# The order of the fallback's flag on VectorE in a fused attention and mixture-of-experts kernel

## Chip, cores and metric

The kernel runs on one core of one Trainium2 chip. The metric is device time in microseconds (us) of one execution, given as the median of several runs. Engines are called by the names of the profile: PE is TensorE's matmul, PEld its weight load, DVE is VectorE, ACT is ScalarE, POOL is GpSimd, SP is SyncE, which here issues the loads and stores.

## What is computed

The reference is attention with a few sink keys and a sliding window, and behind it a mixture of experts that keeps at most `capacity` tokens for each expert:

```
B, H, S, D = 4, 8, 768, 64          # n_sink 4, window 128
scores = q @ k.T / sqrt(D)          # keep: key < n_sink, or 0 <= query - key < window
a = softmax(where(keep, scores, -1e9));   x = a @ v         # x: 3072 tokens x 512
logits = x @ w_gate                 # 8 experts
expert = argmax(logits);  gate = softmax(logits)[expert]
for each expert: keep the 80 tokens (capacity) with the largest gate
    out[token] = gate * (relu(x[token] @ w1[e]) @ w2[e])    # 512 -> 1024 -> 512
```

`n_sink`, `window` and `capacity` come as 64-bit integers in device memory.

## The kernel before, in words

The kernel is built for 4 sinks, a window of 128 and a capacity of up to 80. It computes the output for these numbers, and at the very end it branches to a general and slow version, `any_window`, if a flag says that the numbers are others. The flag needs only the three numbers.

Attention runs in 48 ticks. A tick handles two units; a unit is a block of 128 queries for a pair of heads. The ticks are pipelined by hand: in tick n TensorE computes the scores of tick n (`scores`, L551), turns the probabilities of tick n-1 (L604), and weighs the values of tick n-2 (`weighted`, L639 and L645); in between stand the gate's small matmuls and, in ticks 8 and 9 among others, the turning of finished rows (`rows_turn`, L678). For each unit VectorE copies masked scores inside PSUM (L571) and takes the row maximum `nm` (`softmax`, L578), ScalarE makes the exponentials `prob` (`exps`, L588). GpSimd copies the sinks' probabilities (`sink_probs`, L596 and L597) when the exponentials of a tick are done, and then masks the turned probabilities (`own_probs`, L624, and `before_probs`, L631). The next scores go into the same two PSUM buffers, so TensorE's scores of tick n+1 wait for the exponentials of tick n.

The loop over the ticks stands inside a manual schedule: each engine takes its instructions in the order in which the code writes them. Work that comes up once is put into a calendar: `at((6, "dve end"), f)` calls f in tick 6 behind the softmax of that tick, and "pool" is the place on GpSimd between `sink_probs` and `own_probs`. Entries of the calendar that matter here: `pick_row` is cleared at the end of tick 5 on VectorE (L986), GpSimd makes the picks from it in tick 7 (`make_picks`, L512) and scales the next queries in the same place (`scale_q`, L428), and `read_numbers` stands at the end of tick 6. It turns the integers `ints`, loaded by three small transfers (L489), into floats: a cast (L517), L519, L520, and L521, which writes `prm`. `cut_slots` (tick 9) reads `prm` too.

The flag's five instructions (L1431 to L1434 and L1436, each on one element) are written at the end of the program, behind the manual schedule, so a scheduler puts them where they can run.

Behind the ticks come the ranking of the tokens, the gathers, and from about 203 us the experts' two matrix products, with the weights loaded by SP along the way.

Of the kernel before, what the change touches and what calls it, by code (L numbers as in the profile page):

```python
# [8 lines left out]
F32 = mybir.dt.float32  # L9
F32R = mybir.dt.float32r  # L10
BF16 = mybir.dt.bfloat16
I32 = mybir.dt.int32
I8 = mybir.dt.int8
AF = mybir.ActivationFunctionType
ALU = mybir.AluOpType
# [12 lines left out]
SINK, WIN, CAP = 4, 128, 80  # L28
# [215 lines left out]
def attention_moe(ctx: ExitStack, tc, q, k, v, n_sink, window, w_gate, w1, w2, capacity, q_t, k_t, v_t, vs_t, wg_t, out):  # L244
    nc = tc.nc
    ve, ac, po, pe = nc.vector, nc.scalar, nc.gpsimd, nc.tensor

    const = ctx.enter_context(tc.tile_pool(name="const", bufs=1))
# [79 lines left out]
    with ExitStack() as actx:  # L328
# [159 lines left out]
        for n, a in enumerate((n_sink, window, capacity)):  # L488
            nc.sync.dma_start(ints[:, n, :], a.bitcast(I32).partition_broadcast(P))  # L489
        prm = const.tile([P, 3], F32, name="prm")  # L490

        def make_experts():
            po.iota(e_down, pattern=[[-1, E]], base=E, channel_multiplier=0, allow_small_or_imprecise_dtypes=True)
            po.tensor_scalar(p_bits, e_down, float(8 << 23), float(87 << 23), ALU.mult, ALU.add)
# [20 lines left out]
        def read_numbers():  # L515
            intf = const.tile([P, 3, 2], F32, name="intf")
            ve.tensor_copy(intf, ints)  # L517
            wrap = const.tile([P, 3, 2], F32, name="wrap")
            ve.tensor_scalar(wrap[:, :, 0:1], intf[:, :, 0:1], 0.0, 4294967296.0, ALU.is_lt, ALU.mult)  # L519
            ve.scalar_tensor_tensor(wrap[:, :, 1:2], intf[:, :, 1:2], 4294967296.0, wrap[:, :, 0:1], ALU.mult, ALU.add)  # L520
            ve.tensor_tensor(prm[:, :, None], wrap[:, :, 1:2], intf[:, :, 0:1], ALU.add)  # L521

        def cut_slots():

            past = const.tile([P, CAP], F32, name="past")
            ve.tensor_scalar(past, slot_row, prm[:, 2:3], EMPTY, ALU.is_ge, ALU.mult)
            ve.tensor_tensor(slot_row, slot_row, past, ALU.add)
# [453 lines left out]
        def at(n, f, *args):  # L981
            cal.setdefault(n, []).append((f, args))
# [20 lines left out]
        at((5, "dve end"), ve.memset, pick_row, 1.0)  # L1003
        at((4, "pool"), make_ties)
        at((7, "pool"), make_picks)
        at((6, "dve end"), read_numbers)
        at((9, "dve end"), cut_slots)
        for b in range(B):
            s = b * NPB * NPAIR
            if b + 1 < B:  # L1010
                at(s + 4, load_v, b + 1)
                at(s + 5, load_k, b + 1)
                for n, m in enumerate((0, 2, 1, 3)):
                    at((s + 6 + n, "act end"), round_v, b + 1, m)
                    at((s + (8 if n < 2 else 12), "pool"), split_v, b + 1, m)
# [411 lines left out]
        chain.close()  # L1427

    fast.close()
    flag = const.tile([1, 3], F32, name="flag")  # L1430
    ve.tensor_scalar(flag[:, 0:1], prm[0:1, 0:1], float(SINK), None, ALU.not_equal)  # L1431
    ve.scalar_tensor_tensor(flag[:, 1:2], prm[0:1, 1:2], float(WIN), flag[:, 0:1], ALU.not_equal, ALU.max)
    ve.scalar_tensor_tensor(flag[:, 0:1], prm[0:1, 2:3], 0.0, flag[:, 1:2], ALU.is_lt, ALU.max)
    ve.scalar_tensor_tensor(flag[:, 1:2], prm[0:1, 2:3], float(CAP), flag[:, 0:1], ALU.is_gt, ALU.max)  # L1434
    other = const.tile([1, 1], I32, name="other")
    ve.tensor_copy(other, flag[:, 1:2])  # L1436
    with tc.If(nc.values_load(other, min_val=0, max_val=1) > 0):  # L1437
        any_window(tc, q, k, v, w_gate, w1, w2, prm, ident, out)

# [51 lines left out]
```

## Time and profile before

| what | value |
|---|---|
| median of 3 runs | 296.15 us (295.87 to 297.26) |
| the profiled execution's own time | 294.72 us |
| its span, first to last instruction | 293.0 us |
| mean granted clock of TensorE, share of full | 0.982 |
| busy: PE, DVE, ACT, POOL | 268.8, 171.0, 166.4, 160.5 us |

Busy shares tell which engine has the most work, not which one is late at a given moment. For a step of a pipeline like this one the way to read is: find an idle time of the engine with the most work, see what ended it, and go back through the engine that was waited for until one is found that was busy. The rows of a timeline give start, duration, engine, line, what is written and read, and in brackets an idle time in front with what ended it.

### The profile page before, as it was taken

Reading aid. Unit: us, or ns where it says so; the run is one execution under the profiler, and the core shown is the slowest. Engines: PE = TensorE matmul, PEld = TensorE weight load, DVE = VectorE, ACT = ScalarE, POOL = GpSimd, SP = SyncE. Lnnn points to the kernel's source line nnn. Section 1 sums busy time; section 2 is a strip of 40 time slices with the busy share of each in tenths; the row PEclk is TensorE's granted clock in tenths of the full one; section 3 lists DMA queues with packets and bytes.
Section 4 is the critical chain, followed back from the end, with each engine's and each line's share of the span. In section 5 each row is a group of like instructions: output and inputs, shape, how many; then the busy total and the mean of one; then the engine's idle time right before and its main releaser. Section 6 shows DMA issues by size and latency. Waiting matters only on the chain. (4 is left out here: it accounts for less than half of the span.)

```text
span 293.0 us, 11250 instructions
## 1 busy us (share of the span) xinstructions
PE 268.8 (92%) x4390; PEld 210.5 (72%) x4390; DVE 171.0 (58%) x566; ACT 166.4 (57%) x670; POOL 160.5 (55%) x365
## 2 busy tenths in 40 slices
PE   8889699999999999999989999985999999999991
PEld 3556577676777667667667667643999999998980
DVE  7678878696989888989997897880000000000001
ACT  3867687878987888687578777730112122212210
POOL 5866768758888768769757686735212021001111
PEclk9999799999999999999999999999899999999997
DMA  6989643597880999855184915594989989999811
GB/s 164 371 296 354 241 145 145 213 321 248 273 287 4 293 269 409 333 182 185 63 296 143 347 53 177 173 346 165 311 246 303 298 296 293 312 331 287 279 37 34
DMA packets 33366, 69.76 MB, mean 238 GB/s; under 512 B 4250, under 2 KB 6426, under 8 KB 32922
## 3 DMA queue, kind: packets, MB, share of 16 engines
q1 hardware_dynamic: 32282, 66.34, 66.8%
q0 software_dynamic: 1024, 2.62, 3.0%
q8 instruction: 37, 0.61, 0.9%
q14 instruction: 23, 0.19, 0.2%
HBM read 55.05 MB, written 13.89 MB: 235 GB/s over the span
## 5 line engine op out<-in xcount | busy, mean ns | idle before, releaser
L588 ACT ACTIVATE prob<-sc,nm 128x132 f32<-128x132 f32 (+1 forms) x192 | 68.9, 375 | 12.2 <-DVE nm L578 11.9
L551 PE MATMUL sc<-kv,q 64*64 64x196 f32 (+2 forms) x768 | 48.1, 337 | 9.3 <-ACT prob L588 7.3
L551 PEld LDWEIGHTS sc<-kv,q 64*64 64x64 f32 x768 | 21.5, 133 | 30.7 <-ACT prob L588 19.4
L578 DVE TENSOR_REDUCE nm<-sc 128x2 f32<-128x264 f32 (+1 forms) x96 | 41.4, 431 | 3.3
L571 DVE COPY_PREDICATED sc<-upper,sc 128x256 f32<-128x256 int8 x80 | 33.7, 422 | 14.6 <-PE sc L551 7.5
L616 ACT COPY pt<-pp 128x512 f32<-128x512 f32 x48 | 28.1, 585 | 24.8 <-PE pp L604 19.9
L588 ACT ACTIVATION_READ_ACCUMULATOR prob<-sc,nm 128x1 f32 x192 | 40.3, 210 | 0.0
L1342 DVE COPY xs<-px 128x320 f32<-128x320 f32 x7 | 3.4, 491 | 58.4 <-PE px L1337 51.6
L645 PE MATMUL xp<-pt,kv 128*64 128x128 f32 x384 | 37.4, 287 | 0.0
L624 POOL TENSOR_SCALAR_AFFINE_SELECT own<-pt 128x512 f32<-128x512 f32 (+1 forms) x48 | 27.6, 575 | 11.7 <-ACT pt L616 11.3
L1411 POOL DMA_INDIRECT out_dram<-y,idx x8 | 7.4, 922 | 46.8 <-ACT y L1405 42.9
L604 PE MATMUL pp<-ident,prob 128*128 128x128 f32 x192 | 31.9, 289 | 0.1
L645 PE MATMUL xp<-own,kv 128*64 128x128 f32 x320 | 31.3, 274 | 0.0
L631 POOL TENSOR_SCALAR_AFFINE_SELECT pt<-pt 128x512 f32<-128x512 f32 (+1 forms) x48 | 28.5, 593 | 3.3
L604 PEld LDWEIGHTS pp<-ident,prob 128*128 128x128 f32 x192 | 20.5, 143 | 13.6 <-issue 9.1
L1359 PE MATMUL ph<-xs,w 128*64 128x80 f32 x640 | 27.6, 242 | 0.3 <-issue 0.2
L695 POOL TENSOR_TENSOR xr<-xr,rs 128x512 f32<-128x512 f32 x21 | 22.4, 1067 | 7.7 <-ACT xr L683 7.6
L1359 PEld LDWEIGHTS ph<-xs,w 128*64 128x64 f32 x640 | 25.3, 145 | 0.7 <-issue 0.3
L1377 PE MATMUL py<-h,w 128*64 128x80 f32 x640 | 24.8, 234 | 0.6 <-ACT yt L1388 0.6
L1363 ACT ACTIVATE h<-ph 128x320 f32<-128x320 f32 x16 | 7.0, 437 | 31.4 <-PE ph L1359 31.4
L1377 PEld LDWEIGHTS py<-h,w 128*64 128x64 f32 x640 | 23.1, 137 | 1.6 <-issue 0.8
L645 PEld LDWEIGHTS xp<-pt,kv 128*64 128x64 f32 x384 | 21.4, 138 | 3.5 <-POOL pt L631 0.2
(194 smaller groups left out, 520.7 us busy)
## 6 DMA issues: line engine op xcount, KB each, us to landing
w<-in_moe_w_dram SPq DMA_DIRECT2D x80, 256.0 KB, 4.9
kv_w<-in_moe_w_dram SPq DMA_DIRECT2D x48, 256.0 KB, 4.9
kv<-in_v_t_dram SPq DMA_DIRECT2D x12, 512.0 KB, 8.6
out_dram<-zeros SPq DMA_DIRECT2D x24, 256.0 KB, 5.3
x_rows<-xr SPq DMA_DIRECT2D x24, 256.0 KB, 2.2
q<-in_q_t_dram SPq DMA_DIRECT2D x11, 512.0 KB, 3.8
kv<-in_k_t_dram SPq DMA_DIRECT2D x3, 1584.0 KB, 8.3
kv<-in_k_t_dram SPq DMA_DIRECT2D x2, 528.0 KB, 6.7
```

The lines of the kernel that those rows point to most:

```text
L551: pe.matmul(sc[m * D:(m + 1) * D, h, c0:c1], qs[g][r, hp, q0:q0 + D], ks[b][r, hp, k0 + c0:k0 + c1], start=True, stop=True, skip_group_che ...
L571: ve.copy_predicated(own, upper, sc[:, :, 0:P])
L578: ve.tensor_reduce(out=nm, in_=sc[:, :, lo_c:hi_c], axis=AX.X, op=ALU.max, negate=True)
L588: ac.activation(prob[:, a, h, p0:], sc[:, h, lo_c:hi_c], AF.Exp, bias=nm[:, h:h + 1], scale=1.0, accum_out=ssum[:, n, 2 * hp + h:2 * hp + ...
L604: pe.transpose(pp[:, a, h], prob[:, a, h, SINK:], ident)
L616: ac.copy(pt, st.pop((t, "pp")))
L624: po.affine_select(out=own[:, a0:], in_=pt[:, a0:], pattern=[[0, 2 - a0], [0, 2], [1, P]], compare_op=ALU.is_ge, fill=0.0, base=0, channel ...
L631: po.affine_select(out=pt[:, a0:], in_=pt[:, a0:], pattern=[[0, 2 - a0], [0, 2], [-1, P]], compare_op=ALU.is_gt, fill=0.0, base=0, channel ...
L645: pe.matmul(xp[h * D:(h + 1) * D, a * P:(a + 1) * P], val[:, (2 * hp + h) * D:(2 * hp + h + 1) * D], pr[:, a, h], start=False, stop=(a == ...
L695: po.tensor_tensor(xr, xr, gst[(i0, "rs")][:, n, :, None].to_broadcast([P, H, D]), ALU.mult)
L1359: pe.matmul(ph[m * D:(m + 1) * D, f], columns(0, e, c, fc * P + m * D), x[:, c], start=(c == 0 and not (wide and f)), stop=(c == DC - 1), ...
L1377: pe.matmul(to[m * D:(m + 1) * D, dc], columns(1, e, k, dc * P + m * D), h[:, k], start=(k == 0), stop=(k == HC - 1), skip_group_check=True)
```

## The change

The tiles `flag` and `other` are allocated early, the flag's five instructions become a function `judge_numbers`, and the calendar calls `read_numbers` at the end of tick 5 (behind the clearing of `pick_row`) and `judge_numbers` at the end of tick 6. The instructions themselves are the same ones, and the branch at the end reads the same tile.

```diff
         prm = const.tile([P, 3], F32, name="prm")
+        flag = const.tile([1, 3], F32, name="flag")
+        other = const.tile([1, 1], I32, name="other")
...
+        def judge_numbers():
+            ve.tensor_scalar(flag[:, 0:1], prm[0:1, 0:1], float(SINK), None, ALU.not_equal)
+            ve.scalar_tensor_tensor(flag[:, 1:2], prm[0:1, 1:2], float(WIN), flag[:, 0:1], ALU.not_equal, ALU.max)
+            ve.scalar_tensor_tensor(flag[:, 0:1], prm[0:1, 2:3], 0.0, flag[:, 1:2], ALU.is_lt, ALU.max)
+            ve.scalar_tensor_tensor(flag[:, 1:2], prm[0:1, 2:3], float(CAP), flag[:, 0:1], ALU.is_gt, ALU.max)
+            ve.tensor_copy(other, flag[:, 1:2])
...
-        at((6, "dve end"), read_numbers)
+        at((5, "dve end"), read_numbers)
         at((9, "dve end"), cut_slots)
+        at((6, "dve end"), judge_numbers)
...
     fast.close()
-    flag = const.tile([1, 3], F32, name="flag")
-    ve.tensor_scalar(flag[:, 0:1], prm[0:1, 0:1], float(SINK), None, ALU.not_equal)
-    ve.scalar_tensor_tensor(flag[:, 1:2], prm[0:1, 1:2], float(WIN), flag[:, 0:1], ALU.not_equal, ALU.max)
-    ve.scalar_tensor_tensor(flag[:, 0:1], prm[0:1, 2:3], 0.0, flag[:, 1:2], ALU.is_lt, ALU.max)
-    ve.scalar_tensor_tensor(flag[:, 1:2], prm[0:1, 2:3], float(CAP), flag[:, 0:1], ALU.is_gt, ALU.max)
-    other = const.tile([1, 1], I32, name="other")
-    ve.tensor_copy(other, flag[:, 1:2])
     with tc.If(nc.values_load(other, min_val=0, max_val=1) > 0):
```

In the order of the built programs, VectorE before, from the end of tick 5 on (`nm_6_0` is the row maximum of tick 6, unit 0; the last number of a name counts buffers):

```order
L986 MEMSET pick_row_130 128x1280
L571 COPY_PREDICATED sc_0_156<-upper_160,sc_0_156 128x2x128
L578 TENSOR_REDUCE nm_6_0_495<-sc_0_156 128x2
L571 COPY_PREDICATED sc_1_157<-upper_160,sc_1_157 128x2x128
L578 TENSOR_REDUCE nm_6_1_500<-sc_1_157 128x2
L517 CAST intf_529<-ints_185 128x6
L519 TENSOR_SCALAR wrap_531<-intf_529 128x3
L520 SCALAR_TENSOR_TENSOR wrap_531<-intf_529,wrap_531 128x3
L521 TENSOR_TENSOR prm_189<-wrap_531,intf_529 128x3
L1431 TENSOR_SCALAR flag_5113<-prm_189 1x1
L1432 SCALAR_TENSOR_TENSOR flag_5113<-prm_189,flag_5113 1x1
L1433 SCALAR_TENSOR_TENSOR flag_5113<-prm_189,flag_5113 1x1
```

The same place on VectorE in the changed kernel (its line numbers are its own):

```order
L995 MEMSET pick_row_130 128x1280
L519 CAST intf_474<-ints_185 128x6
L521 TENSOR_SCALAR wrap_476<-intf_474 128x3
L522 SCALAR_TENSOR_TENSOR wrap_476<-intf_474,wrap_476 128x3
L523 TENSOR_TENSOR prm_189<-wrap_476,intf_474 128x3
L580 COPY_PREDICATED sc_0_156<-upper_160,sc_0_156 128x2x128
L587 TENSOR_REDUCE nm_6_0_503<-sc_0_156 128x2
L580 COPY_PREDICATED sc_1_157<-upper_160,sc_1_157 128x2x128
L587 TENSOR_REDUCE nm_6_1_508<-sc_1_157 128x2
L526 TENSOR_SCALAR flag_190<-prm_189 1x1
L527 SCALAR_TENSOR_TENSOR flag_190<-prm_189,flag_190 1x1
L528 SCALAR_TENSOR_TENSOR flag_190<-prm_189,flag_190 1x1
```

The four instructions of the numbers moved from behind the softmax of tick 6 to in front of it; the flag's stand in the same place before and after, ahead of the softmax of tick 7.

GpSimd in ticks 6 and 7, before (masks of tick 5, sinks of tick 6, the picks, the scaling of the third group of queries, masks of tick 6):

```order
L624 AFFINE_SELECT own_5_505<-pt_5_492 128x512
L631 AFFINE_SELECT pt_5_492<-pt_5_492 128x512
L596 CAST stk_0_120<-prob_6_494 128x4x2x4
L597 TENSOR_TENSOR stk_0_120<-prob_6_494,stk_0_120 128x4x2x4
L512 AFFINE_SELECT pick_row_130<-pick_row_130 128x1280
L428 TENSOR_SCALAR q_2_272<-q_2_272 128x1024
L624 AFFINE_SELECT own_6_579<-pt_6_555 128x512
```

And in the changed kernel:

```order
L633 AFFINE_SELECT own_5_513<-pt_5_500 128x512
L640 AFFINE_SELECT pt_5_500<-pt_5_500 128x512
L605 CAST stk_0_120<-prob_6_502 128x4x2x4
L606 TENSOR_TENSOR stk_0_120<-prob_6_502,stk_0_120 128x4x2x4
L514 AFFINE_SELECT pick_row_130<-pick_row_130 128x1280
L428 TENSOR_SCALAR q_2_274<-q_2_274 128x1024
L633 AFFINE_SELECT own_6_586<-pt_6_562 128x512
```

Nothing moved here, and nothing moved on TensorE, ScalarE and SP either.

## Rows read from the trace of the kernel before

**Rows 1.** The page, granted clock in 40 slices, tenths of full speed

```profile
PEclk9999799999999999999999999999899999999997
```

**Rows 2.** Waits: engine, line, releaser; us in all, times, longest

```profile
PE sc L551 <- ACT prob L588: 7.3, 18, 2.1
```

**Rows 3.** Stretches: busy us and instructions of each engine, clock, DMA share, GB/s

```profile
core 0: us, PE busy (x) PEld busy (x) DVE busy (x) ACT busy (x) POOL busy (x), PEclk, DMA share, GB/s
34.00:35.00 1.00, 1.00 (x6) 1.00 (x5) 0.93 (x5) 0.51 (x2) 0.84 (x2) 0.50 0.15 55
...
205.00:293.00 88.00, 80.54 (x2090) 77.20 (x2086) 4.54 (x10) 15.11 (x31) 11.91 (x13) 0.97 0.78 252
```

**Rows 4.** Timeline, PE: the scores of ticks 7 to 10, 15 and 17

```profile
26.85 0.93 PE L551 MATMUL sc<-kv,q 64*64 64x196 f32 x16
...
32.05 0.56 PE L551 MATMUL sc<-kv,q 64*64 64x196 f32 x8 [2.11 <-ACT prob L588]
...
37.23 0.90 PE L551 MATMUL sc<-kv,q 64*64 64x196 f32 x16
...
40.45 0.98 PE L551 MATMUL sc<-kv,q 64*64 64x196 f32 x16
...
57.45 0.45 PE L551 MATMUL sc<-kv,q 64*64 64x64 f32 x8
...
64.15 1.11 PE L551 MATMUL sc<-kv,q 64*64 64x196 f32 x16
```

**Rows 5.** Timeline, DVE: from the end of tick 5 to the softmax of tick 7

```profile
22.49 1.12 DVE L986 MEMSET pick_row<- 128x1280 bf16 x1 [0.21 <-issue]
24.33 0.43 DVE L571 COPY_PREDICATED sc<-upper,sc 128x256 f32<-128x256 int8 x1 [0.72 <-ACT xt L655]
...
25.95 0.53 DVE L517 CAST intf<-ints 128x6 f32<-128x6 int32 x1
26.52 0.17 DVE L519 TENSOR_SCALAR wrap<-intf 128x3 f32<-128x3 f32 x1
26.72 0.48 DVE L520 SCALAR_TENSOR_TENSOR wrap<-intf,wrap 128x3 f32<-128x3 f32 x1
...
27.42 0.14 DVE L1431 TENSOR_SCALAR flag<-prm 1x1 f32<-1x1 f32 x1
27.60 0.21 DVE L1432 SCALAR_TENSOR_TENSOR flag<-prm,flag 1x1 f32<-1x1 f32 x1
27.84 1.24 DVE L1433 SCALAR_TENSOR_TENSOR flag<-prm,flag 1x1 f32<-1x1 f32 x1
29.11 0.98 DVE L1434 SCALAR_TENSOR_TENSOR flag<-prm,flag 1x1 f32<-1x1 f32 x1
...
30.21 0.43 DVE L571 COPY_PREDICATED sc<-upper,sc 128x256 f32<-128x256 int8 x1
```

**Rows 6.** Timeline, POOL: masks of ticks 4 and 5, picks, scaling, mask of tick 6

```profile
23.20 0.64 POOL L631 TENSOR_SCALAR_AFFINE_SELECT pt<-pt 128x512 f32<-128x512 f32 x1
...
25.82 0.64 POOL L624 TENSOR_SCALAR_AFFINE_SELECT own<-pt 128x512 f32<-128x512 f32 x1 [1.37 <-ACT pt L616]
26.52 0.66 POOL L631 TENSOR_SCALAR_AFFINE_SELECT pt<-pt 128x512 f32<-128x512 f32 x1
...
27.75 1.32 POOL L512 TENSOR_SCALAR_AFFINE_SELECT pick_row<-pick_row 128x1280 bf16<-128x1280 bf16 x1
29.05 1.04 POOL L428 TENSOR_SCALAR q<-q 128x1024 f32<-128x1024 f32 x1
30.06 0.63 POOL L624 TENSOR_SCALAR_AFFINE_SELECT own<-pt 128x512 f32<-128x512 f32 x1
```

**Rows 7.** Timeline, ACT: the first exponentials of ticks 6 and 7

```profile
25.64 0.38 ACT L588 ACTIVATE prob<-sc,nm 128x132 f32<-128x132 f32 x1
...
31.14 0.37 ACT L588 ACTIVATE prob<-sc,nm 128x132 f32<-128x132 f32 x1 [2.09 <-DVE nm L578]
```

**Rows 8.** Instructions of tile ints: the last of three issues on SP, and their landing

```profile
L489 SPq DMA_DIRECT2D ints<-in_moe_capacity_dram x1: 327/327/327, 11.5 to 11.5; - x1
...
DMA to landing us min/median/max: 8.3/8.6/9.0
```

## Prediction

> **What bounds the kernel now.** I read the page first, then the waits, then one pause engine by engine. The profiled execution took 294.72 us, 1.72 us of it around a span of 293.0 us; the median of the runs shown is 296.15 us, 1.43 us above the profiled one. TensorE's granted clock is at the full level (2.4 GHz) in nearly all of the span, and one of the few slices that fall short is the sixth, 29.3 to 36.6 us [rows 1]. The list of waits gives score matmuls (L551) that waited for ScalarE's exponentials 18 times, 7.3 us in all, the longest 2.1 us [rows 2]: more than a quarter in one place. TensorE's own rows show where. The scores of tick 7 start at 26.85, those of tick 8 only at 32.05, after 2.11 us of idling; behind it the clock stands at half, 1.2 GHz (0.50 at 34 to 35 us), and tick 8 takes until 37.23 [rows 3, 4]. Tick 9, with the same matmuls at the full clock, takes 37.23 to 40.45, 3.22 us; tick 8 took 5.18 [rows 4].
>
> Back along the pause: ScalarE waited 2.09 us for the row maximum of tick 7 and started the exponentials at 31.14 [rows 7]. VectorE, which makes that maximum, was not idle; it did not start tick 7's softmax before 30.21, although the scores of tick 7 were there at 26.85 + 0.93 = 27.78 [rows 4, 5]. From 25.95 to 30.21 it worked at the four instructions that read the numbers (L517 to L521) and the five of the flag [rows 5]. These are 128x6, 128x3 and 1x1 elements, so their length is not work. The fitting view is GpSimd's rows beside them: the flag's third instruction (27.84 + 1.24 = 29.08) ends with make_picks (27.75 + 1.32 = 29.07), its fourth (29.11 + 0.98 = 30.09) with scale_q (29.05 + 1.04 = 30.09); the cast of the numbers ends at 26.48 with own_probs (26.46), the third number instruction at 27.20 with before_probs (27.18) [rows 5, 6]. So a VectorE instruction with two tiles in SBUF, or a wider cast, that starts beside a running GpSimd instruction ends with that one; the flag's first, with one tile as its input, took 0.14 us and was not held [rows 5].
>
> The Trainium skill says the same in "SBUF — State Buffer", section "Who interferes with whom": the pair of ports that the two engines share is locked for a whole instruction by the one that comes first, and a VectorE instruction with two SBUF inputs, or in a two-port mode, needs it. The trace agrees, to 0.02 us in the four places above. Without that rule the 1.24 and 0.98 us would belong to the instructions themselves and would move with them; that reading is the second rival below.
>
> **The change, part by part.** *Removed behind tick 6:* the four number instructions. They took 25.95 to 27.42 there, 1.47 us [rows 5]. The order shows the flag's five instructions where they stood, between the softmax of tick 6 and that of tick 7, and nothing different on the other four engines. What matters is therefore not where the flag stands but that it starts 1.47 us earlier against GpSimd's row of work.
>
> *Added behind tick 5:* the same four, between the memset of pick_row and the softmax of tick 6. The memset ends at 22.49 + 1.12 = 23.61, and before the softmax of tick 6 at 24.33 VectorE idled 0.72 us [rows 5]. Their price, step by step: the cast starts at 23.64 and is held until before_probs of tick 4 ends at 23.20 + 0.64 = 23.84 [rows 6], so to 23.86; L519 0.17 to 24.06; L520, as short as the flag's second, 0.21, to 24.30, or held by one of GpSimd's short instructions until about 24.5; L521 the rest, 27.20 to 27.42 or 0.22, to 24.5 or 24.7 [rows 5]. The softmax of tick 6 then starts 0.15 to 0.35 us late. At worst cast and L520 are as long as they were, 0.53 and 0.48, and all four take 1.47 us: it starts at 25.1, 0.8 us late. Below nothing this price cannot go, since nothing in front of that softmax is taken away. What is queued behind: tick 6's two copies and two maxima, and for them ScalarE. Its exponentials of tick 6 start at 25.64 with no idle time listed, so ScalarE was busy until then [rows 7], while half of the softmax (24.33 to 25.95) was done by about 25.2 [rows 5]. That slack of 0.4 us hides 0.15 to 0.35; the second unit has less. I take 0.1 us, 0.45 at the other end.
>
> The numbers must be there. The last of their three transfers is issued at 11.5 and lands 8.3 to 9.0 us later, by 20.5 [rows 8], 3.1 us before 23.64. No DMA is moved.
>
> *The flag in its new time:* the softmax of tick 6 ends by 25.95 + 0.35 = 26.3. The flag's first takes 0.14; its second starts at about 26.5 and is held by before_probs of tick 5 to 26.52 + 0.66 = 27.18 at most [rows 6]; the third and fourth at 0.21 each, the fifth at 0.14, with gaps of 0.04: VectorE is free at about 27.9 at the latest, and the scores of tick 7 are there at 27.78. make_picks began at 27.75, and it cannot come earlier: on GpSimd it stands behind sink_probs of tick 6, which waits for tick 6's exponentials, and these come after the very softmax that the flag follows. So the two long GpSimd instructions no longer meet the flag. VectorE's delay of 30.21 - 27.78 = 2.43 us shrinks to 0.1, and with it the 2.11 us of TensorE. GpSimd's two run beside VectorE's copies and reductions of PSUM tiles, of which one ran beside own_probs of tick 6 (30.06 to 30.69) without a hold: 0.43 us at 30.21, as at 24.33 [rows 5, 6].
>
> *The sum.* (1) The pause, 2.11 us. (2) The half clock behind it: 5.18 - 3.22 = 1.96 us [rows 4]. Together 4.07, the upper bound: it takes tick 8 as fast as tick 9, and ticks 9 and 10 found VectorE and GpSimd rested by the pause. The other bound of the two ticks comes from the same place in a later group: ticks 15 and 16 take 57.45 to 64.15, 6.70 us, against 26.85 to 37.23, 10.38 us, now: 3.68 us [rows 4]. Those run with all engines in step, so I take 3.7, less 0.1 for tick 6: a gain of 3.6 us.
>
> *What is late next, and whether it reaches the end.* After tick 8 every queue has the same order, and the loads go out from ticks, so they start earlier too. From 205 us to the end TensorE is busy 80.54 of 88 us, the DMA engines 0.78 of it [rows 3]: the end follows TensorE, not a transfer at a fixed time. I count the gain in full. 296.15 - 3.6 = **292.5 us** (profiled: 294.72 - 3.6 = 291.1, span 289.4).
>
> **The rivals.** *No change: the numbers take the place of the pause.* If the flag still meets make_picks and scale_q, as an instruction that waits for a GpSimd lock might be passed over by the next one in line, softmax 7 stays at 30.2. For it speaks that the flag stays in the same tick; against it that the flag's second, started at 27.60 beside a short GpSimd instruction, ended at 27.81 and was not passed over by make_picks [rows 5, 6]. 296.2 us.
>
> *Part of it: the long instructions are long by themselves.* Then 1.24 and 0.98 go along, the flag ends at 30.21 - 1.47 + 0.2 = 28.9, 1.1 us after the scores; of the pause 2.11 - 1.3 = 0.8 us stays. With the pause cut to 0.8 the clock may fall or not: gain 1.3 to 3.2, about 2, that is 294.2 us. One hold by make_picks alone costs about the same (29.1). Against it: four ends within 0.02 us of GpSimd's.
>
> *Slower: the numbers' transfer.* VectorE now asks for them at 23.64 instead of 25.95. If the last lands at T, softmax 6 starts near T + 0.95, TensorE pauses about T - 23.7, and the half clock costs 1.96 behind it; before, the loss is 4.07, and at a late T at most 0.6 more, if own_probs holds the flag's last too (30.06 + 0.63 = 30.69 for 30.09) [rows 6]. It decides from T of about 26; at 28 the change loses 6.3 against 4.7: 297.8 us. For it: those transfers took over 8 us for 1 KB. Against it: they landed by 20.5 [rows 8], over 5 us ahead of that.
>
> **How the numbers follow.** Forecast (292.5, its own range 291.3 to 293.7, from gains of 4.5 to 2.5 with tick 6 at its dear end) 0.66; part of it 0.17; no change 0.12; slower 0.05. The range of 291.0 to 295.2 takes in the forecast, 4.07 in full with the runs' own scatter, and the part rival down to a gain of 1; it leaves out the other two, 0.17, and a little below. A measurement of this kernel can tell about 0.5%, 1.5 us. Faster by more than that: 0.66 and 0.13 of the part rival, 0.79; within it 0.12 + 0.04 = 0.16; slower 0.05.
>
> **What would show it.** Right: the flag's five instructions take under 1.6 us in all and end before make_picks is half done; softmax 7 starts before 28.2; no TensorE wait over 0.6 us in ticks 6 to 9; clock 1.00 from 28 to 37 us; tick 9's scores at about 33.6. Wrong: an instruction of flag or numbers over 0.8 us, a pause in tick 6 (scores 7 after 27.4), or ticks 7 to 9 repaired and the 3.6 us lost again before 205 us.

## The result

| kernel | median | runs | profiled execution | its span |
|---|---|---|---|---|
| before | 296.35 us | 4 (295.87 to 297.26) | 294.72 us | 293.0 us |
| changed | 292.06 us | 4 (291.52 to 292.34) | 292.34 us | 290.6 us |

The ratio is 0.985, with a 95% interval of 0.9821 to 0.9878: 4.3 us less, where 3.6 were forecast. The two profiled executions differ by 2.4 us only; why is told below, under the repeated traces.

**The profile after.** The granted clock on the page of the changed kernel, in 40 slices, against [rows 1]: the 7 in the fifth slice (29.3 to 36.6 us; the prediction calls it the sixth) is gone, and the short low stretch near the start of the experts is still there (slice 28, slice 29 before).

```profile
PEclk9999999999999999999999999997999999999998
```

TensorE's score matmuls in the timeline of the changed kernel (L560 is L551 of before), ticks 7 to 10 and 12, against [rows 4]:

```profile
26.75 0.93 PE L560 MATMUL sc<-kv,q 64*64 64x196 f32 x16
...
30.02 0.96 PE L560 MATMUL sc<-kv,q 64*64 64x196 f32 x16 [0.19 <-POOL q L428]
...
33.24 1.04 PE L560 MATMUL sc<-kv,q 64*64 64x196 f32 x16
...
36.79 0.90 PE L560 MATMUL sc<-kv,q 64*64 64x196 f32 x16
...
43.41 0.45 PE L560 MATMUL sc<-kv,q 64*64 64x64 f32 x8
```

Tick 7 took 3.27 us instead of 5.20, tick 8 3.22 instead of 5.18. Of the 2.11 us in front of tick 8 there remain 0.19, and these wait for something else: the scaling of the queries on GpSimd.

VectorE in the changed kernel, from the clearing of `pick_row` to the softmax of tick 7 (L519 to L523 are the numbers, L526 to L530 the flag), against [rows 5]:

```profile
22.39 1.12 DVE L995 MEMSET pick_row<- 128x1280 bf16 x1 [0.22 <-issue]
23.43 0.34 DVE L519 CAST intf<-ints 128x6 f32<-128x6 int32 x1
...
24.31 0.41 DVE L580 COPY_PREDICATED sc<-upper,sc 128x256 f32<-128x256 int8 x1
...
25.91 0.13 DVE L526 TENSOR_SCALAR flag<-prm 1x1 f32<-1x1 f32 x1
26.08 0.28 DVE L527 SCALAR_TENSOR_TENSOR flag<-prm,flag 1x1 f32<-1x1 f32 x1
26.39 0.15 DVE L528 SCALAR_TENSOR_TENSOR flag<-prm,flag 1x1 f32<-1x1 f32 x1
26.58 0.49 DVE L529 SCALAR_TENSOR_TENSOR flag<-prm,flag 1x1 f32<-1x1 f32 x1
27.10 0.14 DVE L530 CAST other<-flag 1x1 int32<-1x1 f32 x1
27.45 0.43 DVE L580 COPY_PREDICATED sc<-upper,sc 128x256 f32<-128x256 int8 x1 [0.21 <-ACT xt L664]
```

And GpSimd beside it (masks of tick 5, make_picks, scale_q), against [rows 6]:

```profile
25.72 0.64 POOL L633 TENSOR_SCALAR_AFFINE_SELECT own<-pt 128x512 f32<-128x512 f32 x1 [1.35 <-ACT pt L625]
26.42 0.64 POOL L640 TENSOR_SCALAR_AFFINE_SELECT pt<-pt 128x512 f32<-128x512 f32 x1
...
27.62 1.32 POOL L514 TENSOR_SCALAR_AFFINE_SELECT pick_row<-pick_row 128x1280 bf16<-128x1280 bf16 x1
28.92 1.04 POOL L428 TENSOR_SCALAR q<-q 128x1024 f32<-128x1024 f32 x1
```

The flag takes 1.33 us in all and ends at 27.24, before make_picks begins. It is still held, twice: its second instruction ends at 26.36 with own_probs (25.72 + 0.64), its fourth at 27.07 with before_probs (27.06). The third ran between them in 0.15. The softmax of tick 7 starts at 27.45, with VectorE idle for 0.21 us before it: VectorE waits now and is not waited for. The row puts this wait down to a copy of ScalarE; in the second trace of this kernel (e5) the same 0.21 us are put down to the scores.

### The profile page after: what moved, and what is told of

Read it like the earlier page. It is cut to its first block, busy times and chain, and to the rows that moved or that the text cites. A ratio compares the mean times of both kernels' runs of the same rounds, so it can differ in the third digit from the quotient of the medians.

```text
span 290.6 us, 11250 instructions
## 1 busy us (share of the span) xinstructions
PE 268.0 (92%) x4390; PEld 209.3 (72%) x4390; DVE 168.9 (58%) x566; ACT 166.2 (57%) x670; POOL 160.4 (55%) x365
## 5 line engine op out<-in xcount | busy, mean ns | idle before, releaser
L560 PE MATMUL sc<-kv,q 64*64 64x196 f32 (+2 forms) x768 | 47.9, 337 | 7.4 <-ACT prob L597 5.0
L560 PEld LDWEIGHTS sc<-kv,q 64*64 64x64 f32 x768 | 21.5, 133 | 28.9 <-ACT prob L597 19.1
L625 ACT COPY pt<-pp 128x512 f32<-128x512 f32 x48 | 28.1, 586 | 24.1 <-PE pp L613 19.1
L1369 PE MATMUL ph<-xs,w 128*64 128x80 f32 x640 | 28.3, 241 | 0.1
L1387 PE MATMUL py<-h,w 128*64 128x80 f32 x640 | 25.6, 234 | 1.3 <-issue 0.7
L1369 PEld LDWEIGHTS ph<-xs,w 128*64 128x64 f32 x640 | 26.3, 144 | 0.4 <-DVE xs L1349 0.3
```

Source lines behind the costliest of these rows:

```text
L560: pe.matmul(sc[m * D:(m + 1) * D, h, c0:c1], qs[g][r, hp, q0:q0 + D], ks[b][r, hp, k0 + c0:k0 + c1], start=True, stop=True, skip_group_che ...
L625: ac.copy(pt, st.pop((t, "pp")))
L1369: pe.matmul(ph[m * D:(m + 1) * D, f], columns(0, e, c, fc * P + m * D), x[:, c], start=(c == 0 and not (wide and f)), stop=(c == DC - 1), ...
L1387: pe.matmul(to[m * D:(m + 1) * D, dc], columns(1, e, k, dc * P + m * D), h[:, k], start=(k == 0), stop=(k == HC - 1), skip_group_check=True)
```

## The experiments

Theory (the "lock theory" of the expectations): a VectorE instruction that reads two tiles in SBUF, or the cast of 128x6 elements, waits for the GpSimd instruction that runs when it starts; before, two one-element instructions of the flag waited for make_picks and scale_q, tick 7's softmax was late, TensorE paused, and its clock fell. Rivals: those instructions are long by themselves; the reading of the numbers in tick 6 is what counts; the slow tick 8 has another cause than the clock.

Times of single kernels scatter by about 1% here, so a second measure stands beside them: the time on TensorE from the scores of tick 6 to those of tick 12, from one trace each. It is 24.06 us in the trace of before (47.25 - 23.19) and 20.32 in the changed kernel (43.41, shown above, - 23.09). TensorE's timeline, tick 6 and tick 12 of before, then tick 6 of the changed kernel:

```profile
23.19 1.27 PE L551 MATMUL sc<-kv,q 64*64 64x196 f32 x16 [0.38 <-ACT prob L588]
...
47.25 0.45 PE L551 MATMUL sc<-kv,q 64*64 64x64 f32 x8
```

```profile
23.09 1.27 PE L560 MATMUL sc<-kv,q 64*64 64x196 f32 x16 [0.38 <-ACT prob L597]
```

| run | median, us | ratio to before, 95% | ticks 6 to 12, us | experts, us |
|---|---|---|---|---|
| before, first trace | 296.35 | | 24.06 | 83.9 |
| changed, first trace | 292.06 | 0.985 (0.9821 to 0.9878) | 20.32 | 85.4 |
| e1 before again | 296.04 | 1.0029 (1.0003 to 1.0056) | 24.09 | 86.3 |
| e2 numbers only | 292.12 | 0.9875 (0.983 to 0.992) | 20.34 | 83.7 |
| e3 flag late | 292.42 | 0.9897 (0.9858 to 0.9936) | 20.32 | 85.3 |
| e4 one input | 292.78 | 0.9918 (0.9891 to 0.9946) | 20.46 | 85.3 |
| e5 changed again | 292.44 | 0.9903 (0.987 to 0.9936) | 20.34 | 83.6 |
| e6 GpSimd away | 292.45 | 0.9893 (0.9845 to 0.994) | 20.71 | 86.2 |
| e7 pause filled | 294.16 | 0.9967 (0.9942 to 0.9991) | 22.63 | 83.9 |
| e8 changed, GpSimd away | 292.31 | 0.9886 (0.9853 to 0.9919) | 20.32 | 84.1 |
| e9 probe, two inputs | 290.9 (one run) | | 20.56 | 83.9 |
| e10 probe, one input | 294.39 (one run) | | 20.32 | 86.7 |

("Experts" is the time on TensorE from the first transpose of gathered rows, `px`, to the last matmul of the kernel, from start to start.) The kernel before had medians of 295.34 us beside e1 to e4 and 295.75 beside e5 to e8.

**e1, the kernel before again.** No edit.

> The kernel before, unedited, for a second trace. Lock theory: the hold is fixed by the order of the instructions, so the flag's third and fourth instruction again end within 0.05 us of make_picks and scale_q, softmax 7 starts near 30.2 and TensorE pauses 2.1 us; time 296.3 within 1. What is open: the first trace of this kernel (294.72) is 1.2 us shorter than its fastest timed run. If the experts' part varies from execution to execution by pauses of 0.4 to 0.9 us, as the trace of the changed kernel has two, this trace has some of them and a span of 294 to 295.5; if the first trace was usual, the span is 293.0 again.

The ticks repeat to 0.03 us (24.09 against 24.06): the pause in front of tick 8 is 2.12 us, tick 8 takes 5.19. The experts' part does not repeat, 86.3 us against 83.9, and with it the span, 296.1 us, lies above the 294 to 295.5 that were expected. Its timeline has two pauses of TensorE in the second product of experts 1 and 2 that the first trace lacks, at the places where the changed kernel's first trace has them too. The timeline of e1, and under it that of the changed kernel:

```profile
228.10 0.64 PE L1377 MATMUL py<-h,w 128*64 128x80 f32 x12 [0.36 <-issue]
...
238.87 0.67 PE L1377 MATMUL py<-h,w 128*64 128x80 f32 x13 [0.38 <-issue]
```

```profile
223.71 0.67 PE L1387 MATMUL py<-h,w 128*64 128x80 f32 x13 [0.38 <-issue]
...
234.51 0.69 PE L1387 MATMUL py<-h,w 128*64 128x80 f32 x13 [0.36 <-issue]
```

So the first trace of before was a short execution, and the two spans that happen to stand side by side (293.0 and 290.6) understate the gain. Compared with itself, the kernel before also came out at 1.0029 with an interval that leaves out 1: differences of 0.3% are not read as anything below.

**e2, the numbers alone.** The flag stays at the end of the code, where the scheduler places it.

```diff
-        at((6, "dve end"), read_numbers)
+        at((5, "dve end"), read_numbers)
```

> Only the numbers are read a tick earlier; the flag stays where the scheduler puts it, which then sets its first two instructions between the copies and maxima of tick 6. Lock theory: the flag is done before make_picks, the pause of 2.1 us is gone; the two instructions in between delay tick 6's maxima by 0.2 to 0.6 us, of which ScalarE's slack hides some; 292.0 to 292.8. If the flag's instructions are long by themselves (1.24 and 0.98 us), softmax 7 starts near 28.9 and the time is about 294.2. If the fixed place of the flag is what matters, about 296.

Measured 292.12 us, ticks 6 to 12 in 20.34. The scheduler sets the flag's first two instructions among the copies and maxima of tick 6; in the timeline of e2, VectorE, they cost 0.14 each, and the softmax of tick 7 starts in time:

```profile
24.65 0.14 DVE L1431 TENSOR_SCALAR flag<-prm 1x1 f32<-1x1 f32 x1
...
25.44 0.14 DVE L1432 SCALAR_TENSOR_TENSOR flag<-prm,flag 1x1 f32<-1x1 f32 x1
...
27.46 0.43 DVE L571 COPY_PREDICATED sc<-upper,sc 128x256 f32<-128x256 int8 x1 [0.73 <-PE sc L551]
```

The fixed place of the flag adds nothing that can be measured; the earlier reading of the numbers gives the whole gain by itself, because the flag then starts earlier too.

**e3, the flag alone, far away.** The numbers stay in tick 6; the flag goes behind the selection of tokens. The edit is shown against the changed kernel.

```diff
-        at((5, "dve end"), read_numbers)
+        at((6, "dve end"), read_numbers)
-        at((6, "dve end"), judge_numbers)
...
             ve.tensor_copy(idx, idxf)
+            judge_numbers()
```

> The numbers stay in tick 6 as before, the flag goes to the stretch after the selection of tokens, where VectorE waits for the gathers. Lock theory: the numbers cost 1.5 us behind softmax 6 as before and end near 27.4, softmax 7 starts near 27.5, no pause, full clock: as the changed kernel, 292.1 within 0.7. If the reading of the numbers in tick 6 is what delays tick 7, the pause stays and the time is 296.

Measured 292.42 us, 20.32. The numbers end 0.1 us earlier on the clock of the trace, as the whole tick does, and the softmax of tick 7 still starts in time (VectorE, e3):

```profile
27.13 0.16 DVE L523 TENSOR_TENSOR prm<-wrap,intf 128x3 f32<-128x3 f32 x1
27.45 0.43 DVE L580 COPY_PREDICATED sc<-upper,sc 128x256 f32<-128x256 int8 x1 [0.16 <-ACT xt L664]
```

Reading the numbers in tick 6 does no harm by itself. What has to leave is the flag's stretch beside the two long GpSimd instructions; the change does that by letting the flag start earlier.

**e4, the same order, other instructions.** The order of before; only the form of the flag's instructions differs, so that each reads one tile.

```diff
-    ve.scalar_tensor_tensor(flag[:, 1:2], prm[0:1, 1:2], float(WIN), flag[:, 0:1], ALU.not_equal, ALU.max)
-    ve.scalar_tensor_tensor(flag[:, 0:1], prm[0:1, 2:3], 0.0, flag[:, 1:2], ALU.is_lt, ALU.max)
-    ve.scalar_tensor_tensor(flag[:, 1:2], prm[0:1, 2:3], float(CAP), flag[:, 0:1], ALU.is_gt, ALU.max)
+    ve.tensor_scalar(flag[:, 1:2], prm[0:1, 1:2], float(WIN), None, ALU.not_equal)
+    ve.tensor_scalar(flag[:, 2:3], prm[0:1, 2:3], 0.0, None, ALU.is_lt)
+    ve.tensor_scalar(flag[:, 3:4], prm[0:1, 2:3], float(CAP), None, ALU.is_gt)
+    ve.tensor_reduce(out=flag[:, 4:5], in_=flag[:, 0:4], axis=AX.X, op=ALU.max)
```

> The order of before, with the flag made of instructions that have one tile as input (four comparisons of one element, a maximum over four, a cast: six instead of five). Lock theory: none of them is held by GpSimd, each takes 0.13 to 0.2 us, softmax 7 starts at 28.4 to 28.7, the pause shrinks from 2.1 to 0.3 to 0.6 us and the clock stays full: 292.3 to 293.3. If small instructions are long there for a reason of their own, or the order alone counts, nothing changes: 296.

Measured 292.78 us, 20.46. VectorE and, under it, GpSimd in the timeline of e4:

```profile
27.34 0.14 DVE L1431 TENSOR_SCALAR flag<-prm 1x1 f32<-1x1 f32 x1
27.41 0.13 DVE L1432 TENSOR_SCALAR flag<-prm 1x1 f32<-1x1 f32 x1
27.47 0.13 DVE L1433 TENSOR_SCALAR flag<-prm 1x1 f32<-1x1 f32 x1
27.53 0.13 DVE L1434 TENSOR_SCALAR flag<-prm 1x1 f32<-1x1 f32 x1
27.69 0.15 DVE L1435 TENSOR_REDUCE flag<-flag 1x1 f32<-1x4 f32 x1
27.87 0.14 DVE L1437 CAST other<-flag 1x1 int32<-1x1 f32 x1
27.95 0.43 DVE L571 COPY_PREDICATED sc<-upper,sc 128x256 f32<-128x256 int8 x1
```

```profile
27.66 1.33 POOL L512 TENSOR_SCALAR_AFFINE_SELECT pick_row<-pick_row 128x1280 bf16<-128x1280 bf16 x1
```

make_picks runs from 27.66 to 28.99, and the maximum at 27.69 and the cast at 27.87 take 0.15 and 0.14 beside it. The softmax follows 0.61 us behind the flag's first instruction, where it followed 2.79 us behind [rows 5]. The expected start of the softmax, 28.4 to 28.7, was too late: these four comparisons, with no wait between them, start 0.06 to 0.07 us apart. In the order of before, the form alone brings the gain. The form differs in two ways, though: each instruction reads one tile, and the comparisons do not wait for one another, so that they were all under way before make_picks began. Only the maximum and the cast ran beside make_picks; the number of inputs by itself is tried in e9 and e10.

**e6, GpSimd's instructions away.** The kernel before; VectorE's order and instructions are untouched.

```diff
-        at((7, "pool"), make_picks)
+        at((10, "pool"), make_picks)
...
-            at(((g - 1) * NPAIR + 3, "pool"), scale_q, g)
+            at(((g - 1) * NPAIR + (2 if g == 2 else 3), "pool"), scale_q, g)
```

> The order of before on VectorE; only GpSimd's two long instructions leave the flag: make_picks goes from tick 7 to tick 10, the scaling of the third group of queries from tick 7 to tick 6. Lock theory: the flag's instructions meet at most the masks (0.64 us each) and end by 28.9 instead of 30.2; softmax 7 starts at 28.2 to 29.0, the pause is 0.3 to 0.9 us, and with a full clock the time is 292.5 to 294. If small instructions are long by themselves, nothing changes on VectorE: 296.

Measured 292.45 us, 20.71. The flag's third and fourth instructions, on VectorE in e6, and what GpSimd does meanwhile: it idles from 27.82 to 29.14.

```profile
27.86 0.15 DVE L1433 SCALAR_TENSOR_TENSOR flag<-prm,flag 1x1 f32<-1x1 f32 x1
28.05 0.15 DVE L1434 SCALAR_TENSOR_TENSOR flag<-prm,flag 1x1 f32<-1x1 f32 x1
...
28.31 0.43 DVE L571 COPY_PREDICATED sc<-upper,sc 128x256 f32<-128x256 int8 x1
```

```profile
27.57 0.25 POOL L597 TENSOR_TENSOR stk<-prob,stk 128x32 f32<-128x32 f32 x1
29.14 0.65 POOL L624 TENSOR_SCALAR_AFFINE_SELECT own<-pt 128x512 f32<-128x512 f32 x1 [1.32 <-ACT pt L616]
```

The same two instructions that took 1.24 and 0.98 us [rows 5] take 0.15 each. They are not long by themselves; that rival is out. The ticks take 0.4 us more here than in the changed kernel: the flag still stands in front of the softmax, which starts at 28.31, and TensorE's scores of tick 8 wait 0.15 and 0.24 us for the exponentials.

**e9 and e10, a probe.** The changed kernel with one instruction of one element more, between the two units of tick 7's softmax, beside make_picks. Nobody reads its result.

```diff
+                        if n == 7 and a == 0:
+                            ve.scalar_tensor_tensor(probe, prm[0:1, 2:3], 0.0, flag[:, 1:2], ALU.is_lt, ALU.max)   # e9
+                            ve.tensor_scalar(probe, prm[0:1, 2:3], 0.0, None, ALU.is_lt)                           # e10
```

> The changed kernel with one more instruction of one element, whose result nobody reads, between the two units of tick 7's softmax on VectorE; it has two tiles in SBUF as inputs. It starts near 28.3, beside make_picks (27.62 to 28.94). Lock theory: it ends at 28.9 to 29.0 with make_picks, 0.6 to 0.7 us instead of 0.15, and the second unit's copy starts near 29.0 instead of 28.27. If small instructions are long only behind the reading of the numbers, it takes 0.15 to 0.2 us.

> The same with one tile as input. Lock theory: 0.13 to 0.14 us, not held although make_picks runs, and the second unit's copy starts at 28.3 to 28.4. If any VectorE instruction between SBUF tiles is held by GpSimd, it takes 0.6 us like the other.

VectorE in e9 and make_picks on GpSimd there, which ends at 29.06:

```profile
28.38 0.68 DVE L1116 SCALAR_TENSOR_TENSOR probe<-prm,flag 1x1 f32<-1x1 f32 x1
29.00 0.41 DVE L581 COPY_PREDICATED sc<-upper,sc 128x256 f32<-128x256 int8 x1
```

```profile
27.74 1.32 POOL L515 TENSOR_SCALAR_AFFINE_SELECT pick_row<-pick_row 128x1280 bf16<-128x1280 bf16 x1
```

VectorE in e10, and under it make_picks, which runs from 27.72 to 29.04:

```profile
28.37 0.13 DVE L1116 TENSOR_SCALAR probe<-prm 1x1 f32<-1x1 f32 x1
28.43 0.41 DVE L581 COPY_PREDICATED sc<-upper,sc 128x256 f32<-128x256 int8 x1
```

```profile
27.72 1.32 POOL L515 TENSOR_SCALAR_AFFINE_SELECT pick_row<-pick_row 128x1280 bf16<-128x1280 bf16 x1
```

Same place, same size: 0.68 us with two tiles as input, 0.13 with one, both as expected. The 0.5 us that the held probe adds cost 0.24 us over ticks 6 to 12 (20.56 against 20.32). The two times (290.9 and 294.39, one run each) do not bear on this, since the experts' part differs by 2.8 us between them.

The Trainium skill's "SBUF — State Buffer", section "Who interferes with whom", has both halves: two SBUF inputs contend with a GpSimd instruction that reads SBUF, one input outside the two-port modes does not. The probes agree: beside the same make_picks, 0.68 us in e9 and 0.13 in e10.

**e7, the pause filled.** The kernel before with matmuls that nobody reads where TensorE pauses.

```diff
         at((9, "dve end"), cut_slots)
+        at((7, "pe end"), warm, 8)
```

> The kernel before with eight more matmuls that nobody reads (128x512, about 2 us in all) at the end of tick 7 on TensorE, where it pauses. The pause as such stays: the scores of tick 8 start at 32.0 to 32.3. If the half clock behind the pause costs what the sum says (1.96 us), the clock stays at full speed, tick 8 takes 3.2 to 3.4 us instead of 5.2 and the time is 294.2 to 294.7. If the slow tick 8 has another reason (engines out of step), it stays at 5 us and the time at 296.3.

Measured 294.16 us. TensorE's timeline in e7, then the stretch from 34 to 36 us in e7 and in e1 (busy us of PE, PEld, DVE, ACT, POOL, then the granted clock, the DMA share and GB/s):

```profile
30.00 1.90 PE L875 MATMUL warm<-ones_bf 128*128 128x512 bf16 x8
32.18 0.56 PE L551 MATMUL sc<-kv,q 64*64 64x196 f32 x8 [0.29 <-issue]
...
35.76 1.04 PE L551 MATMUL sc<-kv,q 64*64 64x196 f32 x16
...
39.32 0.90 PE L551 MATMUL sc<-kv,q 64*64 64x196 f32 x16
```

```profile
34.00:36.00 2.00, 2.00 (x31) 1.73 (x30) 1.84 (x12) 1.86 (x10) 1.86 (x4) 1.00 0.09 32
```

```profile
34.00:36.00 2.00, 2.00 (x14) 1.84 (x14) 1.83 (x13) 1.76 (x8) 1.86 (x4) 0.50 0.16 61
```

The scores of tick 8 start as late as before, but the clock stays at the full level and tick 8 takes 3.58 us instead of 5.19. Ticks 6 to 12 take 22.63 us: 1.46 us less than in e1. That is the worth of the clock, and the rest down to the changed kernel's 20.33, 2.30 us, is the pause. The other cause of the slow tick 8 is out as the main one: of its 5.19 us the clock gives back 1.61. But 3.58 is more than the 3.2 to 3.4 that were expected, and the forecast price of the clock, 1.96, was 0.5 too high. In e1 the clock did not fall in the pause itself: it stands at 1.00 up to 33 us, 0.9 us after the scores of tick 8 have begun, at 0.86 from 33 to 34, and at 0.50 from 34 to 37.

**e8, the changed kernel with GpSimd's instructions away.** The edit of e6 on the changed kernel.

> The changed kernel with make_picks in tick 10 and the scaling of the third group of queries in tick 6. In the changed kernel the scores of tick 8 wait 0.19 us for that scaling and GpSimd runs about a microsecond behind in ticks 8 and 9 (scores of tick 10 at 36.79, a tick of 3.55 us). If GpSimd's lag costs there, 0.2 to 0.5 us come back: 291.6 to 291.9. If not, 292.1. The scaling may now hold the numbers of tick 6: not over 0.3 us.

Measured 292.31 us, and e5, the changed kernel again, 292.44 beside it: no difference. The scores of tick 8 do start 0.26 us earlier (29.76), but tick 8 then takes 3.47 and those of tick 10 stand at 36.78 as in the changed kernel (36.79). GpSimd's lag was not what ends tick 9; what does was not tried.

**e5, the changed kernel again.** No edit.

> The changed kernel, unedited, for a second trace. Ticks 5 to 12 as in its first trace to 0.1 us (scores of tick 12 near 43.4); time 292.1 within 0.7. If the pauses of TensorE in the experts' part (0.9 us twice) are fixed by the change, they stand at the same instructions again; if they vary from execution to execution, they stand elsewhere or are gone, and the span lies between 288.7 and 290.6.

Ticks 6 to 12 take 20.34 us, and TensorE's two pauses stand in the second products of experts 1 and 2 again (222.91 and 233.69); the experts' part is 83.6 us, with a span of 289.4. These pauses are in every trace but the first of before and those of the two probes, with the change or without. What they wait for is not in the profile (they are put down to "issue"), and it was not tried.

These two pauses are only one part of what varies. The probe e10 lacks them but has three others, in the first products; this is the first, in e10's timeline of TensorE, and the others are 0.62 and 0.78 us:

```profile
219.04 3.33 PE L1372 MATMUL ph<-xs,kv_w 128*64 128x80 f32 x89 [1.66 <-issue]
```

A second part is the clock. Its short low stretch lies in the first 12 us of the experts in the first traces of both kernels (mean 0.86), and ahead of them in e5, where the experts have it at 1.00: the same kernel with the same two pauses takes 85.4 us in one trace and 83.6 in the other. With the mean at 0.86, the experts take 83.9 us without the pauses (e9), 85.4 with them (the changed kernel's first trace) and 86.7 with the three others (e10). So neither the two pauses nor their absence tells a long execution from a short one.

## Why the prediction was right

*Where the time was lost:* as read. The chain from GpSimd's long instructions over VectorE's softmax and ScalarE to TensorE's pause and its clock is what e4, e6, e7, e9 and e10 take apart, link by link. The signs that the prediction named came: the flag takes 1.33 us, the softmax of tick 7 starts at 27.45, no wait of TensorE in ticks 6 to 9 is over 0.38 us, the clock is 1.00 from 28 to 37 us, and tick 9's scores start at 33.24.

*The numbers in tick 5:* forecast 0.15 to 0.35 us of delay for the softmax of tick 6 and 0.1 behind it. It starts 1.22 us after its scores (24.31 - 23.09), against 1.14 before (24.33 - 23.19) [rows 5], so 0.08 late; ScalarE's exponentials start 0.10 us earlier on the clock of the trace, as the whole tick does. The price was nothing: tick 6 takes 3.66 us on TensorE in both. The cast began before the memset had ended (23.43 against 23.51), a step that the sum did not have.

*The flag in its new time:* forecast one hold, of the flag's second instruction by before_probs up to 27.18, and VectorE free at 27.9 at the latest; two were held, the second to 26.36 by own_probs and the fourth to 27.07 by before_probs, and VectorE was free at 27.24. The reason given, that make_picks stands behind the exponentials of the softmax that the flag follows, held: it began at 27.62. The prediction had the scores of tick 7 there only at 27.78, when the last of them ends; the first unit's softmax starts at 27.45, before that, so VectorE was late before by more than the 2.43 us of the text.

*The pause and the clock:* 2.11 and 1.96 us were the terms; e7 gives 2.30 and 1.46. The sum is close to what was forecast: 3.7 taken near the lower of the bounds 4.07 and 3.68, less 0.1 for tick 6, and 3.74 measured over ticks 6 to 12 (24.06 - 20.32). In part that is luck: the pause was taken too small, the clock too dear, and the 0.1 for tick 6 was not lost. The upper bound was off where the prediction expected it: tick 8 is now as fast as tick 9 was (3.22), but tick 9 takes 3.55. In e7 too ticks 8 and 9 take 3.58 and 3.56. The reason given, that VectorE and GpSimd no longer come rested out of a pause, is not shown; e8, with GpSimd's two long instructions away, leaves tick 9 at 3.55. One bound of the range is a slip: a gain of 4.5 us gives 291.65, not 291.3.

*What is late next:* not foreseen was the 0.19 us wait for scale_q in front of tick 8; e8 shows that it costs nothing in the end.

*Whether it reaches the end:* ticks 12 to 47 take 130.25 us before and 130.28 after: nothing is lost there. Between the scores of tick 47 and the first expert the traces differ by half a microsecond either way (25.6 and 25.6 before, 25.2 and 25.7 after), with the gathers. The experts' part varies by 3 us from one execution to the next, more than what any step of the sum was worth. The difference between 3.7 and the 4.3 us of the medians is small against that; in the later runs (e5) the ratio was 0.9903 (0.987 to 0.9936), about 2.9 us.

*What was overlooked:* SP's queue. It reads the flag into a register long before the end, and in the first trace of before it waited for it, where the prediction saw nothing different on the other four engines. The row of SP's waits before names the row maximum, but the read starts at 30.3, just behind the flag's last instruction (30.13 to 30.27). In the changed kernel it starts at 27.3. SP's wait before, and the read in the changed kernel:

```profile
SPq L1437 <- DVE nm L578: 4.8, 1, 4.8
```

```profile
L1440 SPq TENSOR_LOAD <-other x1: 482/482/482, 27.3 to 27.3; - x1
```

Behind it in SP's queue stands a store of finished rows that goes out at 39.65 us before and at 36.19 in the changed kernel, so the 3 us by which SP is freed earlier were worth nothing here. Even in e3, where the read waits until 195.4 us, the next load goes out at 198.15, as in the changed kernel (198.14).

*The rivals:* no change fell with the result itself, since the flag ends at 27.24 and make_picks begins at 27.62; long instructions fell with e6, e9 and e10; the late numbers did not come up: the cast starts with no idle time before it, before and after.

## What to carry to other kernels

A small VectorE instruction that takes many times its usual length is a sign to lay GpSimd's rows beside it: if both end together, the cure is another moment, another form with a single tile as input, or another moment for GpSimd's instruction, and all three were worth nearly the same here: 20.3, 20.5 and 20.7 us over ticks 6 to 12, against 24.1. A pause of TensorE may have to be priced with the clock behind it (here 2.30 and 1.46 us), and that price is best taken from a run that fills the pause, not from the slow tick alone. Where one part of a kernel varies by more than the change is worth, compare the stretch that the change touches across two traces of each kernel before spans are compared.

## What the runs showed of the hardware that was not expected

- The hold needs no data to speak of: one element on one partition waited 1.24 us for a GpSimd instruction over 128x1280 elements (before), and 0.68 us in e9.
- A held VectorE instruction can get in between two GpSimd instructions in a row: in the changed kernel the fourth of the flag ended at 27.07 with the one it met (27.06), although GpSimd's next began at 27.13. It does not always: in the trace of before, an instruction of `cut_slots` (L526) that started at 39.55, 0.07 us before the end of the GpSimd instruction beside it (39.62), ended at 40.27, with GpSimd's next one (39.58 to 40.22).
- In e4 four comparisons of one element, with one input each and no wait between them, started within 0.19 us.
- The experts' part of one and the same kernel took 83.9 and 86.3 us in two executions. The pauses of TensorE and the place of the low clock both vary; what sets them is open.
